# An attention and feed-forward kernel: a new table for the order and the engines of 1349 steps

## The chip, the cores and the metric

The kernel runs on one core of a Trainium2 chip. The metric is device microseconds (us) of one execution. The core has a matrix engine (PE, with its weight loads told apart as PEld), three engines for elementwise work (DVE, ACT and POOL), a sequencer that mostly issues DMA transfers (SP), and 16 DMA engines that all queues share. Each engine takes its instructions in the order in which the program gives them; between engines, semaphores hold an instruction until its operands are there.

## The reference

Linear attention with position weights comes first, then a feed-forward layer with the gate h * cos(h):

```python
r = np.maximum(x, 0.0)
phi = np.concatenate([r * cos_w, r * sin_w], axis=-1)     # for q and for k
kv = np.einsum('bhsf,bhsd->bhfd', k_p, v)
num = np.einsum('bhsf,bhfd->bhsd', q_p, kv)
den = np.einsum('bhsf,bhf->bhs', q_p, np.sum(k_p, axis=2))[..., None] + 1e-06
x = (num / den).transpose(0, 2, 1, 3).reshape(4608, 512)
h = x @ w_in                                              # 512 x 2048
out = (h * np.cos(h)) @ w_out                             # 2048 x 512
```

There are 8 batches of 8 heads, 576 rows each, 64 wide; all inputs and the output are float32.

## The kernel before

The 576 rows of a batch are laid out as 128 partitions by four and a half tiles. Tiles 0 to 3 give the 512 columns of one chunk of the feed-forward layer; the half tiles of two batches share one tile, and these rests make a ninth chunk of 512. A batch passes through these stages:

- load (L316, L319): each of k, q and v of a batch comes in by two DMA transfers on SP's queue, one of 640 KB and one of 512 KB, here called its halves (the first two batches have v in four). The raw tiles km, qm and vm exist once, so a load waits until the previous batch's work on them is done.
- prep (L343 on ACT, L344 on DVE): relu times the cosine or sine weight, from km or qm into the tile KQ, ten for k and ten for q in each batch. ENGS says which of the two engines makes each one.
- cast_v (L359 on POOL): v to 16 bits.
- kv (L370 on PE): the products of k and v into the PSUM tile ATT, copied to kvz.
- q_dma (L409 on SP): a DMA transpose of one tile of q from KQ into qT; five per batch, here called qT0 to qT4. The batches 0 and 1 use PE instead (q_pe, L399).
- num (L431 on PE, L447 to L451 on DVE): numerator and denominator, and their quotient x.
- x_dma (L481 on SP): a DMA transpose of x into xT (or xR for the rests). Batches 0 to 2 use PE (L471).
- layer 1 (L528, L560 and L664 on PE): x @ w_in, with the gate as sine on ACT (L501, L687) and product on DVE (L503, L693). L664 is part of a scheme with seven products for eight, whose sums of x (XS, L621) and of the weights (WS, L600) are made by DVE and whose partial results go through Z (L672 on ACT, L676 on DVE).
- layer 2 (L783 and L858 on PE): the product with w_out, copied to ost by ACT (L869) or added by DVE (L880), and stored by POOL (L729, L742, L746; the last chunk by SP and ACT).

Layer 1 of a chunk, layer 2 of the chunk before and the attention of a later batch run interleaved. Weights come at the start by POOL's DMA (w_in L953, w_out L967). Small copies on POOL (hold, L947, L957, L972, L979) hold back a DMA until another one has landed.

No scheduler decides the order when the program is built. Every step is registered once, with its dependencies; then a planned start (STARTS, in hundredths of a microsecond) and an engine letter (ENGS) are read from two tables:

```python
order = sorted(range(len(st)), key=lambda n: (STARTS[n], n))
...
s["fn"] = {self.LETTER[e]: o[3] for e, o in s["opts"].items()}[ENGS[s["n"]]]
return [st[n] for n in order]
```

The instructions are issued in this order, and what an engine gets of them is its queue. A planned start is thus nothing but a key to sort by. The other figures that a step is registered with (its length, its due time, the size and rate of its transfer, and how late it may land) were used by the search that made the tables; the function that runs here does not read them. In addition, steps on DVE and POOL that are marked with port=True wait for the one before them in the order when it is on the other of these two engines.

Of the kernel before, what the change touches and what calls it, by code (L numbers as in the profile page):

```python
# [11 lines left out]
ALU = mybir.AluOpType  # L12
# [6 lines left out]
    0, 53, 106, 0, 0, 71, 136, 201, 266, 331, 396, 461, 940, 1080, 1170, 990, 1662, 1904, 2064,  # L19
    1934, 607, 607, 797, 886, 733, 691, 888, 1346, 649, 669, 751, 817, 775, 731, 842, 1481, 934,  # L20
    997, 1064, 1039, 1163, 1081, 1216, 1123, 1002, 955, 940, 1191, 1126, 1258, 1225, 1165, 1284,
    1309, 1335, 1272, 1309, 1302, 1378, 1441, 1452, 1547, 1510, 1674, 1560, 1810, 1845, 1523, 1535,
    1559, 1646, 1736, 1770, 1833, 1797, 1894, 1845, 2022, 2084, 1711, 1723, 1779, 1912, 1947, 1935,
    2034, 2104, 2045, 2144, 2214, 2271, 2370, 2440, 2183, 2283, 2353, 2358, 2457, 2527, 2532, 2631,
    2701, 2445, 2544, 2614, 2619, 2719, 2789, 2794, 2893, 2995, 2707, 2806, 2934, 2881, 2980, 3056,
    3101, 3200, 3270, 3014, 3125, 3195, 3188, 3312, 3382, 3363, 3486, 3556, 3275, 3536, 3617, 2892,
    2850, 2968, 3030, 1752, 1792, 1857, 2044, 2084, 2952, 3689, 3719, 3809, 2024, 1642, 3017, 3082,
    3147, 3212, 3485, 3362, 4076, 3586, 3443, 3648, 3678, 3424, 3331, 3250, 3720, 3772, 3884, 3956,
    3762, 3710, 4148, 4218, 3846, 3884, 4102, 4194, 3888, 3983, 4363, 4490, 3804, 4119, 4318, 4375,
    4118, 3946, 4050, 4045, 3930, 4025, 4082, 4143, 4181, 4169, 4194, 4256, 4330, 4447, 4434, 4561,  # L30
    4684, 4719, 4410, 4422, 4446, 4657, 4819, 4720, 4707, 4784, 4948, 5010, 4645, 4632, 4669, 4925,
    4960, 4971, 5343, 5379, 5627, 5662, 3539, 3834, 3712, 4390, 3930, 4440, 4460, 4769, 4753, 5003,
    5455, 5671, 7278, 7188, 5170, 5816, 5824, 6060, 9378, 7368, 5083, 5182, 5526, 4996, 5095, 5178,
    5737, 5923, 5999, 5650, 5749, 5877, 5367, 5605, 5938, 6171, 6271, 6341, 5997, 6097, 6167, 6084,
    6209, 6279, 6470, 6629, 6786, 6383, 6517, 6587, 6557, 6741, 6847, 6879, 7027, 7116, 6756, 6865,
    6950, 6978, 7077, 7177, 7287, 7413, 7532, 7065, 7363, 7593, 4889, 5064, 8120, 9186, 4136, 4201,
    4331, 4266, 4396, 4461, 5232, 5356, 5484, 5281, 5480, 5239, 5418, 5294, 5323, 5542, 6030, 5860,
    5970, 6321, 6259, 6395, 5732, 5587, 5792, 5799, 5861, 5943, 5774, 6147, 6295, 5629, 5973, 6420,
    6228, 6035, 6675, 6644, 6657, 6681, 6856, 6915, 6843, 6966, 7011, 7177, 7313, 7153, 7165, 7238,
    7399, 7463, 7387, 7375, 7427, 7597, 7631, 6463, 7667, 7842, 6669, 7200, 7513, 7422, 7509, 7781,  # L40
    8356, 8262, 8522, 9043, 8002, 8917, 9155, 9288, 9375, 9726, 9487, 9661, 9787, 9866, 11601, 9834,
    9922, 10021, 11781, 11691, 7743, 7867, 7998, 7830, 7979, 8059, 7916, 8091, 8234, 8089, 8188,
    8295, 8176, 8362, 8512, 8349, 8474, 8573, 8435, 8534, 8634, 8609, 8707, 8837, 8806, 8993, 9064,
    8720, 8819, 8898, 9091, 9205, 9405, 9177, 9379, 9604, 9005, 9553, 9665, 9575, 9958, 10044, 9748,
    9846, 9983, 10034, 10195, 10295, 5562, 5627, 6545, 6610, 6165, 6230, 6965, 7385, 7189, 7127,
    6679, 6455, 7251, 7343, 6567, 6908, 7078, 6968, 7458, 7619, 7681, 8584, 7681, 7917, 7999, 8029,
    7956, 8124, 7743, 8238, 8320, 7805, 8300, 8575, 8412, 8644, 8791, 8708, 8695, 8732, 8916, 8893,
    8905, 8959, 9082, 9276, 9263, 9300, 9423, 9463, 9475, 9499, 9622, 10009, 10120, 10157, 10655,
    6402, 9125, 9848, 9922, 10483, 10691, 10988, 10145, 10487, 10601, 10877, 10977, 11453, 12461,
    11164, 11337, 11630, 11623, 11953, 12326, 11778, 12281, 12697, 12664, 12752, 13128, 14121,  # L50
    14211, 12926, 13057, 13250, 14301, 14614, 10262, 10389, 10356, 10597, 10232, 10307, 10275,
    10422, 10501, 10630, 10443, 10551, 10660, 10716, 10704, 10805, 10834, 10927, 11006, 11112,
    11064, 11294, 11392, 10574, 10766, 10866, 10747, 11244, 11331, 11493, 11680, 11783, 11251,
    11518, 11680, 11108, 11406, 11424, 11514, 11780, 12225, 11579, 11730, 11735, 11830, 11865,
    11949, 11909, 12010, 12240, 12347, 12040, 12128, 12286, 12108, 12550, 12636, 12194, 12500,
    12575, 12578, 12836, 12973, 12368, 12724, 12912, 7445, 7510, 8510, 8726, 7575, 8445, 9317, 8869,
    8470, 8931, 9429, 9491, 9603, 9093, 9255, 8757, 9578, 9468, 9318, 10381, 10319, 10878, 10133,
    9665, 10215, 9896, 10071, 10340, 9727, 10105, 10530, 10816, 10357, 10963, 10245, 10651, 11153,
    10964, 11151, 11226, 11349, 11468, 11480, 11575, 12092, 11722, 11710, 11844, 11967, 12096,
    12083, 12120, 12243, 13189, 13364, 13539, 13578, 13690, 13794, 13491, 13777, 13994, 14372,  # L60
    13951, 14094, 14299, 14566, 14853, 15094, 14436, 14678, 15228, 15248, 15422, 15666, 17419,
    17219, 15509, 15640, 15876, 15946, 16036, 12800, 12879, 12846, 13095, 12839, 12894, 12882,
    13034, 13362, 13653, 13013, 13069, 13144, 13200, 13188, 13303, 13404, 13478, 13596, 13819,
    13447, 13906, 14116, 13231, 13744, 13933, 13318, 13956, 14055, 14281, 14846, 14924, 13865,
    14560, 14652, 14050, 14106, 14237, 14311, 14734, 14985, 14194, 14249, 14392, 14448, 14523,
    14591, 14766, 14821, 15008, 15114, 14809, 14896, 15046, 15113, 15211, 15434, 14940, 15261,
    15373, 15336, 15702, 15877, 15026, 15311, 15938, 9747, 9877, 11088, 10898, 9812, 10465, 12071,
    12066, 12004, 10938, 11942, 11456, 11741, 11568, 11880, 11344, 11491, 11321, 11431, 12454,
    12516, 13412, 12944, 12774, 13026, 13300, 13119, 13382, 12438, 12662, 12744, 12178, 12758,
    13637, 12600, 12376, 14454, 13678, 13665, 13714, 13837, 14181, 14038, 14206, 14329, 14380,  # L70
    14367, 14486, 14961, 14654, 14666, 14713, 14836, 15224, 15199, 15561, 16086, 15999, 16146,
    16443, 16254, 16441, 16544, 16341, 16572, 16671, 17857, 16659, 16746, 16845, 16915, 17129,
    17161, 17862, 17987, 17317, 17516, 17801, 18080, 18167, 18534, 19296, 19206, 17949, 18255,
    18584, 18654, 18744, 19116, 20038, 15528, 15495, 15844, 16113, 15596, 15652, 15727, 15783,
    16110, 16382, 15938, 16060, 15895, 15950, 16210, 16321, 16068, 16260, 16408, 16557, 16528,
    16594, 16732, 15982, 16494, 16671, 16112, 16721, 16793, 16877, 17223, 17409, 17075, 17173,
    17243, 16833, 16957, 16963, 17027, 17441, 17796, 17032, 17273, 17273, 17329, 17473, 17735,
    17404, 17632, 17851, 17971, 18037, 18092, 18162, 17603, 17937, 18085, 17690, 18142, 18223,
    18385, 18484, 18631, 17776, 18254, 18509, 12433, 12368, 13507, 13572, 12869, 13151, 13844,
    14672, 13534, 15144, 15289, 14610, 14006, 14349, 13682, 13472, 14504, 14011, 13951, 15833,  # L80
    15771, 16000, 15361, 14946, 15443, 14784, 14498, 15086, 15814, 15752, 15896, 15331, 14882,
    16496, 16222, 16284, 17336, 16198, 16428, 16854, 16977, 17007, 17019, 17088, 17211, 17249,
    17261, 17304, 17733, 17448, 17460, 17485, 17608, 18725, 18961, 19374, 18944, 19316, 19415,
    18856, 19229, 19670, 20203, 19558, 19689, 19788, 19948, 19858, 20130, 20217, 20316, 19987,
    20373, 20940, 20787, 20874, 21110, 21574, 21484, 21048, 21135, 21234, 21394, 21304, 22607,
    22697, 18284, 18359, 18434, 18692, 18342, 18428, 18472, 18570, 18746, 18839, 18639, 18696,
    18683, 18796, 18813, 18900, 19031, 19086, 19165, 19488, 19099, 19251, 19707, 18727, 18918,
    19208, 19143, 19620, 19768, 19801, 20192, 20500, 19403, 19838, 19934, 19490, 19545, 19931,
    19995, 20242, 20647, 19645, 19720, 20086, 20142, 19887, 20317, 20304, 20378, 20579, 20708,
# [93 lines left out]
def kernel(  # L183
# [9 lines left out]
    nc = tc.nc  # L193
# [85 lines left out]
    LATE_BY, LATE_W = (0.0, 1.0, 3.0, 1.0), 0.6  # L279
# [3 lines left out]
    pl = Plan()  # L283
# [843 lines left out]
```

## Time and profile before

| what | us |
|---|---|
| median of 3 runs (lowest, highest) | 283.99 (283.96, 285.28) |
| the profiled execution | 284.86 |
| its span, from the first to the last instruction | 282.8 |
| PE busy | 270.5 (96%) |
| DVE busy | 241.8 (85%) |
| ACT busy | 208.9 (74%) |
| share of PE in the chain that ended last | 74% |
| share of DMA in that chain | 16% |
| transfers of SP's queue, as a share of 16 engines' span | 61.5% |
| transfers of POOL's queue, likewise | 29.6% |

The busy time of an engine is counted from its instructions; issuing a DMA is not counted as busy on SP, but the time that the issue takes is in the timeline. The list of waits tells for every engine and line what ended its idle time. A wait that PE doesn't see costs nothing by itself. The granted clock of PE was 1.00 throughout.

### The profile page before, as it was taken

How to read it: one execution, taken by the hardware profiler on the slowest of the kernel's cores; microseconds unless marked ns; L12 is line 12 of the kernel's file. 1: busy time of each engine (PE TensorE's matmuls, PEld its weight loads, DVE VectorE, ACT ScalarE, POOL GpSimd, SP SyncE). 2: the span in 40 equal slices, each digit the busy share in tenths (PEclk: the TensorE clock that was granted, in tenths of full speed). 3: DMA queues.
4: the chain of work that ended last, by engine and by line, in shares of the span. 5: the costliest groups of instructions: out<-in, count | busy, mean ns of one | idle time of the engine just before them, and what ended most of it. 6: DMA issues, size and time to landing. Idle time of an engine off the chain costs nothing.

```text
span 282.8 us, 6698 instructions
## 1 busy us (share of the span) xinstructions
PE 270.5 (96%) x2643; PEld 210.2 (74%) x2643; DVE 241.8 (85%) x451; ACT 208.9 (74%) x363; POOL 57.8 (20%) x87
## 2 busy tenths in 40 slices
PE   6789999999999899999999999999999999999994
PEld 2468947679955577777777787787778888776883
DVE  2975897999997789998999899999999879977752
ACT  2766897898998887798989697996555687676220
POOL 1412020030500400410042023205201360330410
PEclk9999999999999999999999999999999999999999
DMA  6999999999999979999999999959583975694424
GB/s 214 302 206 253 268 258 244 352 255 214 239 294 205 286 185 297 183 312 235 271 232 322 110 333 251 231 97 205 104 140 105 188 141 74 167 126 79 101 82 154
DMA packets 83390, 58.79 MB, mean 208 GB/s; under 512 B 46368, under 2 KB 80416, under 8 KB 83360
## 3 DMA queue, kind: packets, MB, share of 16 engines
q1 hardware_dynamic: 72128, 40.77, 61.5%
q0 software_dynamic: 10496, 17.04, 29.6%
q10 hardware_dynamic: 736, 0.57, 0.6%
q8 instruction: 20, 0.33, 0.5%
q14 instruction: 10, 0.08, 0.1%
HBM read 36.74 MB, written 11.80 MB: 172 GB/s over the span
## 4 chain that ended last, share of the span: by engine, by line
PE 74%; DMA 16%; ACT 4%; DVE 3%; issue 2%; POOL 0%; SPq 0%; DVEq 0%; POOLq 0%
PE M L858 28%; PE M L664 10%; PE M L560 10%; PE M L528 9%; DMA qT<-KQ 8%; PE TR L664 4%; PE M L783 4%; DMA w_in_sb<-in_moe_w_in_dram 3%; PE TR L560 3%; DMA km<-in_k_dram 3%; PE ATT L431 3%; PE ATT L370 2%; ACT KQ L343 2%; DMA xT<-x 2%; ACT ch L501 1%
## 5 line engine op out<-in xcount | busy, mean ns | idle before, releaser
L858 PEld LDWEIGHTS <-gT 128*128 128x128 f16 x560 | 54.2, 98 | 8.7
L501 ACT ACTIVATE ch<-M 128x512 f32<-128x512 f32 x85 | 49.6, 595 | 13.1 <-PE M L560 5.3
L503 DVE TENSOR_TENSOR gT<-M,ch 128x512 f16<-128x512 f32 x78 | 51.4, 683 | 8.1 <-ACT ch L501 8.0
L858 PE MATMUL M<-w_out_sb,gT 128*128 128x256 f16 x448 | 56.0, 273 | 0.0
L343 ACT ACTIVATE KQ<-qm,CS 128x512 f16<-128x512 f32 x55 | 37.9, 718 | 6.3 <-DMA qm<-in_q_dram 4.2
L560 PE MATMUL M<-xT,w_in_sb 128*128 128x512 f16 x160 | 38.8, 379 | 0.4 <-DVE gT L503 0.4
L343 ACT ACTIVATE KQ<-km,CS 128x512 f16<-128x512 f32 x55 | 37.6, 724 | 1.3 <-DMA km<-in_k_dram 1.3
L869 ACT ACTIVATE ost<-M 128x512 f32<-128x512 f32 x41 | 24.1, 597 | 18.4 <-PE M L858 14.5
L560 PEld LDWEIGHTS <-w_in_sb 128*128 128x128 f16 x224 | 21.4, 98 | 18.5 <-issue 0.6
L359 POOL CAST V<-vm 128x1024 f16<-128x1024 f32 (+1 forms) x18 | 16.0, 912 | 90.8 <-DVE KQ L344 27.7
L858 PE MATMUL M<-T,S 128*128 128x256 f16 x256 | 32.3, 272 | 0.0
L528 PE MATMUL M<-xT,w_in_sb 128*128 128x256 f16 x256 | 30.0, 273 | 0.6 <-DVE gT L503 0.3
L858 PEld LDWEIGHTS <-S 128*128 128x128 f16 x256 | 24.6, 98 | 4.0
L528 PEld LDWEIGHTS <-w_in_sb 128*128 128x128 f16 x256 | 24.5, 98 | 3.9 <-DVE gT L503 0.6
L664 PEld LDWEIGHTS <-w_in_sb 128*128 128x128 f16 x216 | 20.6, 98 | 3.4 <-issue 0.2
L451 DVE TENSOR_TENSOR x<-ATT,rec 128x512 f16<-128x512 f32 x32 | 22.1, 691 | 1.1
L431 PEld LDWEIGHTS <-qT 128*128 128x128 f16 x320 | 15.5, 98 | 5.4 <-DMA qT<-KQ 1.7
L729 POOL DMA_DIRECT2D out_dram<-ost x20 | 11.1, 560 | 35.3 <-ACT ost L869 19.0
L676 DVE TENSOR_TENSOR Z<-M,Z 128x512 f32<-128x512 f32 x26 | 17.7, 683 | 0.6 <-PE M L664 0.6
L672 ACT ACTIVATE Z<-M 128x512 f32<-128x512 f32 x22 | 13.1, 598 | 6.8 <-PE M L664 4.2
L431 PE MATMUL ATT<-kvz,qT 128*128 128x65 f16 x288 | 16.0, 194 | 1.7 <-DMA qT<-KQ 0.9
L664 PEld LDWEIGHTS <-WS 128*128 128x128 f16 x144 | 13.7, 98 | 4.9 <-DVE XS L621 0.9
(145 smaller groups left out, 460.6 us busy)
## 6 DMA issues: line engine op xcount, KB each, us to landing
out_dram<-ost POOLq DMA_DIRECT2D x38, 256.0 KB, 4.6
qm<-in_q_dram SPq DMA_DIRECT2D x8, 640.0 KB, 6.4
km<-in_k_dram SPq DMA_DIRECT2D x8, 640.0 KB, 7.4
qm<-in_q_dram SPq DMA_DIRECT2D x8, 512.0 KB, 6.4
km<-in_k_dram SPq DMA_DIRECT2D x8, 512.0 KB, 6.2
vm<-in_v_dram SPq DMA_DIRECT2D x6, 640.0 KB, 6.1
vm<-in_v_dram SPq DMA_DIRECT2D x6, 512.0 KB, 6.5
w_in_sb<-in_moe_w_in_dram POOLq DMA_DIRECT2D x4, 512.0 KB, 9.2
```

Source lines behind the costliest of these rows:

```text
L343: fn = {"ACT": lambda: nc.scalar.activation(out=out_, in_=in_, func=AF.Relu, scale=sc), "DVE": lambda: nc.vector.tensor_scalar(out=out_, i ...
L359: "POOL": lambda: nc.gpsimd.tensor_copy(out=out_, in_=in_)}
L431: nc.tensor.matmul(bank[hb][:, hh * D1:(hh + 1) * D1], lhsT=a[:, h, :], rhs=z[:, h, :], start=(i == 0), stop=(i == len(parts) - 1))
L451: nc.vector.tensor_tensor(out=split(x16[n][:, hs, :], k), in0=A[:, :, :, 0:D], in1=split(rec[n][:, hs], k).unsqueeze(3).broadcast_to((P, k ...
L501: act(0.5, due, lambda: nc.scalar.activation(out=ch[c], in_=bank, func=AF.Sin, bias=math.pi / 2.0, scale=1.0), [key], [("ch", c)])
L503: mul(due, 0.61, lambda q: q.tensor_tensor(out=dst, in0=bank if len(dst.shape) == 2 else bank.rearrange("p (j s) -> p j s", j=dst.shape[1] ...
L528: nc.tensor.matmul(M1[m][:, jj * 2 * P:(jj + 1) * 2 * P], lhsT=w_in_sb[:, cc, j * P:(j + 1) * P], rhs=X[:, cc, ts], start=(cc == 0), stop= ...
L560: nc.tensor.matmul(M, lhsT=w_in_sb[:, cc, j * P:(j + 1) * P], rhs=X[:, cc, :], start=(cc == 0), stop=(cc == NCT - 1))
L664: nc.tensor.matmul(bank[0][:, j * TH:(j + 1) * TH], lhsT=a(cc, j), rhs=b[:, cc, :], start=(first and j == 0 and cc == 0), stop=(last and j ...
L676: dve(0.61, due + 0.3, lambda: nc.vector.tensor_tensor(out=dst, in0=bank[0], in1=dst, op=ALU.add), [bank[1], key], [key])
L858: nc.tensor.matmul(bank[0][:, tt * MH:(tt + 1) * MH], lhsT=a[:, j, tt * P:(tt + 1) * P], rhs=b[:, j, :], start=(first and (apart or tt == ...
L869: act(0.5, due, lambda: nc.scalar.activation(out=dst, in_=view(bank), func=AF.Copy), [bank[1]], dk)
```

## The change

Two tables change, and with them the order on each engine; the functions register the same 1349 steps, and the program has the same instructions. Of the steps, 38 preparations change their engine: 22 from DVE to ACT and 16 from ACT to DVE. PE keeps 422 steps, POOL 81 and SP 111, in another order. The changed figures of length (0.9 to 0.55 and 1.2 to 0.9 for a DMA that POOL issues, 0.65 to 0.62 for a store by SP) and LATE_BY are those that the search read. A limit on what SP's queue can hold was part of the search and does not stand in the code.

```diff
 STARTS = (
-    0, 53, 106, 0, 0, 71, 136, 201, 266, 331, 396, 461, 940, 1080, 1170, 990, 1662, 1904, 2064,
...
+    53, 106, 0, 0, 74, 139, 204, 269, 334, 399, 464, 543, 1050, 1190, 1280, 1100, 1370, 2014, 2134,
...
 ENGS = (
...
-    "ADPADPADPADPADPADDDDDSSSSSSAADDADAADAGGGPPADDSAASDASDASDASPPDPAPPDPAPPDPAPPDPADDDPPAPPDDPP"
+    "ADPADPADPADPADPADDDDDSSSSSSDDADADAADAGGGPPADASAASDASAASAASPPDPAPPDPAPPDPAPPDPADDDPPAPPDDPP"
...
-    LATE_BY, LATE_W = (0.0, 1.0, 3.0, 1.0), 0.6
+    LATE_BY, LATE_W = (0.0, 0.8, 1.8, 0.5), 0.6
...
-        pl.add(eng, 0.9 if eng == "POOL" else 0.65, 0, due, lambda: q.dma_start(out=dst, in_=src_), keys, [], dma=(nb, 355.0))
+        pl.add(eng, 0.55 if eng == "POOL" else 0.62, 0, due, lambda: q.dma_start(out=dst, in_=src_), keys, [], dma=(nb, 355.0))
```

The order on SP's queue from the loads of batch 4 to the last transpose of batch 3 shows the kind of change (kA and kB, qA and qB, vA and vB are the halves of batch 4; the qT of the first column are those of batch 3, but for qT4 of batch 2 where it says so):

```
before: qT4 of batch 2, kA, kB, vA, qT0, qT1, qT2, vB, qA, qT3, qB, qT4, four xT
after:  kB, qT4 of batch 2, qT0, vA, kA, qT1, vB, qT2, qA, qT3, qB, qT4, four xT
```

On POOL, the four loads of w_in now follow each other at once, and the four stores of chunk 0 (L729) stand together around the last cast of v of batch 3; before, three stood there and the fourth stood with the casts of batch 4.

## The prediction

> **What bounds the kernel now.** I read the page first, then the table of stretches, then the chain of waits, and last what PE and SP waited for between 74 and 140 us. All times are those of one profiled execution: 284.86 us, of which the span is 282.8 and 2.06 lie around it. It is 0.87 above the median of the three runs, 283.99.
>
> ```profile
> PE 270.5 (96%) x2643; PEld 210.2 (74%) x2643; DVE 241.8 (85%) x451; ACT 208.9 (74%) x363; POOL 57.8 (20%) x87
> ```
>
> PE is the bound, busy for 96% of the span. The stretches show where the rest lies (columns: PE, PEld, DVE, ACT, POOL busy with instructions in brackets, clock, DMA share, GB/s).
>
> ```profile
> 60.00:80.00 20.00, 20.00 (x262) 17.25 (x260) 18.70 (x36) 17.85 (x34) 5.95 (x9) 1.00 1.05 230
> 80.00:100.00 20.00, 18.59 (x144) 11.55 (x142) 16.99 (x33) 17.81 (x33) 3.15 (x4) 1.00 1.11 281
> 100.00:120.00 20.00, 19.37 (x206) 15.11 (x205) 18.63 (x35) 15.94 (x29) 3.28 (x5) 1.00 0.97 213
> 120.00:140.00 20.00, 19.45 (x195) 15.01 (x193) 18.65 (x33) 18.42 (x34) 1.38 (x3) 1.00 1.14 278
> 140.00:180.00 40.00, 40.00 (x416) 32.40 (x414) 37.84 (x72) 34.37 (x60) 10.41 (x16) 1.00 1.17 258
> 180.00:220.00 40.00, 40.00 (x385) 31.55 (x383) 38.48 (x67) 28.05 (x50) 8.16 (x12) 1.00 0.75 132
> ```
>
> PE idles in the head (to 36 us), at the tail (after 277.1), and between 80 and 140 us; outside these it is full, so there no order of the other engines can gain anything. The idle of 80 to 140 us is four waits, told by the list of waits:
>
> ```profile
> PE ATT L431 <- DMA qT<-KQ: 0.9, 1, 0.9
> PE M L664 <- DVE XS L621: 0.6, 1, 0.6
> PE M L664 <- ACT Z L672: 0.5, 1, 0.5
> ...
> PE M L560 <- DVE gT L503: 0.4, 1, 0.4
> ```
>
> In order of time they end at 87.42 (L560), 97.28 (L431), 107.87 and 134.41 us (L664) and last 0.44, 0.91, 0.63 and 0.55. Behind each stands a transfer of SP's queue. DVE came late to the first for a half of k (the same list: DVE KQ L344 waited 0.9 for km, to 86.28 us), the second is a transposed q, the third a transposed x (DVE XS L621 waited 1.0), the fourth began with ACT waiting 1.3 for a qT. SP's rows show why:
>
> ```profile
> 71.46 2.06 SPq L409 DMA_TRANSPOSE qT<-KQ  x1
> ...
> 75.71 1.55 SPq L316 DMA_DIRECT2D km<-in_k_dram  x1
> ...
> 80.69 8.08 SPq L409 DMA_TRANSPOSE qT<-KQ  x3
> ...
> 90.29 3.16 SPq L409 DMA_TRANSPOSE qT<-KQ  x1
> ...
> 96.64 3.08 SPq L481 DMA_TRANSPOSE xT<-x  x2
> ...
> 132.31 1.24 SPq L409 DMA_TRANSPOSE qT<-KQ  x1
> ```
>
> A transpose is issued in 1.24 us where nothing stands ahead of it (last line), and often in 2 to 4 us from 64 to 125 us (8.08 for three): SP can't hand over the next one until earlier transfers have gone. The DMA engines' share there is 1.11 and 1.14.
>
> **The change part by part.** *The numbers in the code.* Only STARTS and ENGS act on the program: run() sorts by STARTS. The costs, LATE_BY and the room of the queue act on nothing that is built. Cost 0; PE has the same 2643 matmuls.
>
> *What can be won.* Each wait also empties PE's pipe: a 128x256 matmul lasts 273 ns, but eight take 0.87 us, 109 ns each, so a gap costs 0.16 more than it shows. The four are worth 0.60, 1.07, 0.79 and 0.71, together 3.17 us.
>
> *Engines.* Of the head preparations 22 go from DVE to ACT and 16 back: ACT gains 6 x 0.72 = 4.3 us, DVE loses 6 x 0.49 = 2.9. I cost this at 0. ACT's idle 74 us cover it; without that cover (17.81 of 20 busy from 80 to 100 us) a preparation on ACT holds up the sines of L501 queued behind it, 0.72 each.
>
> *Head.* POOL issues the fourth w_in load with the others (11 to 14 us, before 17.44), and the holds of the next raw loads follow it; the second q half and the v loads are issued up to 7 us earlier, behind k loads that are still under way. What PE waits for stays: w_in (first L528 at 20.75) and w_out (L783 at 36.17). I take 0. Bounds: a gain of 0.6 (the waits of 0.28 and 0.32 at 20.75 and 23.20), a loss of 0.74 (one POOL issue of w_in more ahead).
>
> *First wait (0.60).* The qT4 of batch 2 goes from 71.46 to behind the first half of the next k, and the second half of that k, before next to the first, now follows qT4, qT0 and a v half. Before, the halves landed 9.4 and 10.4 us after their issue, the last at 86.1. Two more transfers (qT0, v) now precede the last. In the full queue from 80.69 to 96.53 eight transfers were issued in 15.84 us, 1.98 each; unhindered, a transpose takes 1.24 and a load 0.60. So that half lands at 86.3 + 1.84 = 88.1 to 86.3 + 3.96 = 90.2. The new table sets its first use (now ACT) 1.96 us later than before; a group of eight matmuls counts 0.87 there as in the rows, so I read this as 1.96 us of PE work done first. Against the old wait that is -0.1 to +2.0; I take +0.6, below the middle, since ACT's other preparations can run ahead. Behind it in ACT's queue stand a copy of L869 and the sines that DVE's L503 needs, and PE waits for L503. This wait: 1.2, from 0.5 to 2.6.
>
> *Second wait (1.07).* It is for qT3 of batch 3. Ahead of it in SP's queue since 71 us are the same nine transfers, in another order, and all four stores of POOL now stand at 72 to 74 us, where three stood (the fourth was at 95.60). PE comes later to it by the first wait's growth. I take 0.5; bounds 0 and 1.07 + 0.93 = 2.0 (256 KB at 281 GB/s for the fourth store).
>
> *Third wait (0.79).* The x transposes keep their place behind qT4; only the loads behind them change order. They start when DVE's x is there. I take 0.2, near the row of an unhindered xT (2.8 to 3.3 us to land), bounds 0 and 0.79.
>
> *Fourth wait (0.71).* qT4 of batch 4 goes behind the first x transpose, three more x transposes follow it, then the next k. It landed 8.82 us after its issue; the median is 5.5. The table leaves 6.2 between issue and the preparation that overwrites its source. I take 0.3; bounds 0 and 8.82 - 6.2 = 2.6, halved to 1.3 since ACT is behind PE by less than its wait.
>
> *Later.* From 140 us PE never waited. SP's transfers move by up to 9 us in the table there, a k half of batch 6 again parts from its twin. New waits: 0.2, bounds 0 and 1.0. The tail keeps its 5.7 us from 277.1 on.
>
> *Sum.* 1.2 + 0.5 + 0.2 + 0.3 + 0.2 = 2.4 in place of 3.17: 0.8 gained, 284.06 for an execution like the profiled one, and 0.87 less for the median: 283.2.
>
> While the three stores were under way (8.7 to 9.4 us from issue to landing), the qT issued at 71.46 took 10.2 us to land; the k halves of the batch before, with no store beside them, took 4.1 and 5.2. [...]
>
> **The rivals.** *SP is on time.* The new order leaves more work between issue and use; then only the first wait's lower end, 0.5, stays: 283.99 - 2.67 = 281.3. For it: all four waits are SP's, and the queue is not full after 125 us. Against: the DMA share of 1.11, which an order can't lower.
>
> *Nothing moves.* The DMA engines are full, not SP's handing over; the same bytes land when they did and the waits keep their sum of 3.17: 284.0. For it: the nine transfers ahead of qT3, and the burst of four stores, which may take back at qT3 what is won before it. [...] Against: between 100 and 120 us the share is 0.97, and a wait is there all the same.
>
> *Slower: the parted k.* The second half of k lands at 90.2, ACT stands still 2.0 longer than DVE did, and the other three waits stay: 283.99 + 2.0 = 286.0. It decides when that half lands later than 86.3 + 1.96 = 88.2, and passes 0.5% from 89.7 on. For it: 9.4 and 10.4 us to landing in this very place. Against: ACT has other work that could fill the time, if its order lets it.
>
> **How the numbers follow.** Half a per cent (1.42 us) is about what a measurement of this kernel can tell from no change: faster is below 282.57, slower above 285.41. My sum 0.35 (its own range 282.2 to 284.2, a sixth of it below 282.57), SP on time 0.22, nothing moves 0.25, the parted k 0.18. Faster: 0.22 + 0.06 + 0.02 = 0.30. Slower: 0.16 + 0.01 = 0.17. Same: 0.53. The range leaves half of the fast rival below 281.5 and half of the slow one above 285.8.
>
> **What would show it.** Each step by its wait: at about 88 us ACT L343 waiting for km (right) or DVE (wrong); qT landing for L431 near 97; XS L621 waiting under 0.4 for xT; no PE idle from 140 to 277 us. If SP's transposes between 76 and 97 us take 1.3 us each, SP is on time and I am too slow; if PE idles in the head or in a stage that was full, I am too fast.

## The result and the profile after

| | median, us | range, us | ratio to the kernel before, 95% interval |
|---|---|---|---|
| before, 22 runs | 284.37 | 281.02 to 286.70 | |
| changed, 22 runs | 286.42 | 284.28 to 288.47 | 1.009 (1.0065 to 1.0114) |

The changed kernel is 0.9% slower. Forecast were 283.2, a range of 281.5 to 285.8, and a chance of 0.17 for slower. (Intervals here leave out executions more than 1.5% above the fastest of their kernel; medians and means keep them.)

The profiled execution of the changed kernel took 284.28 us (span 282.5): the shortest of its 22. Read alone, it agrees with the forecast (284.06 for an execution like the profiled one). Its busy line, and its stretches in the columns shown for before:

```profile
PE 270.9 (96%) x2643; PEld 210.1 (74%) x2643; DVE 241.0 (85%) x445; ACT 213.0 (75%) x369; POOL 57.7 (20%) x87
```

```profile
60.00:80.00 20.00, 19.96 (x260) 17.20 (x259) 18.08 (x36) 18.21 (x33) 5.40 (x8) 1.00 1.08 288
80.00:100.00 20.00, 19.68 (x158) 12.47 (x157) 18.77 (x34) 17.52 (x33) 2.61 (x3) 1.00 1.10 241
100.00:120.00 20.00, 19.16 (x200) 15.05 (x199) 18.20 (x33) 17.89 (x32) 0.95 (x2) 1.00 1.03 198
120.00:140.00 20.00, 19.93 (x200) 15.54 (x199) 19.28 (x35) 18.14 (x32) 4.31 (x7) 1.00 1.11 287
140.00:180.00 40.00, 39.36 (x407) 31.41 (x405) 36.28 (x69) 35.03 (x61) 9.95 (x15) 1.00 1.10 248
```

PE's idle time from 80 to 140 us fell from 2.59 to 1.23 us, and 0.64 is new between 140 and 180. The list of waits names what PE waited for; the first two lines lie in the head:

```profile
PE M L399 <- ACT KQ L343: 2.6, 1, 2.6
PE ATT L942 <- POOL S L928: 1.3, 1, 1.3
PE ATT L431 <- DMA qT<-KQ: 1.2, 2, 0.8
PE M L858 <- ACT ost L869: 0.6, 1, 0.6
```

The timeline of SP's queue, and ACT's use of the parted half of k:

```profile
75.69 5.22 SPq L409 DMA_TRANSPOSE qT<-KQ  x2
...
81.67 0.63 SPq L319 DMA_DIRECT2D km<-in_k_dram  x1
...
104.71 7.99 SPq L409 DMA_TRANSPOSE qT<-KQ  x3
```

```profile
86.98 1.33 ACT L343 ACTIVATE KQ<-km,CS 128x512 f16<-128x512 f32 x2 [0.32 <-DMA km<-in_k_dram]
```

SP needs 2.6 us for a transpose in these rows, against 2.7 in the row of 80.69 before, and 1.5 to 3.5 between 82 and 95 us, so SP hands them over about as slowly as it did. But what PE needs lands in time more often: the half of k issued at 81.67 is there at 86.98, after a wait of ACT of 0.32, and PE doesn't see it. So this profile shows a gain, and 22 executions show a loss. The experiments look for what this profile leaves out.

### The profile page after: what moved, and what is told of

It is laid out like the page before. It is cut to its first block, busy times and chain, and to the rows that moved or that the text cites. A ratio compares the mean times of both kernels' runs of the same rounds, so it can differ in the third digit from the quotient of the medians.

```text
span 282.5 us, 6678 instructions
## 1 busy us (share of the span) xinstructions
PE 270.9 (96%) x2643; PEld 210.1 (74%) x2643; DVE 241.0 (85%) x445; ACT 213.0 (75%) x369; POOL 57.7 (20%) x87
## 4 chain that ended last, share of the span: by engine, by line
PE 47%; DMA 4%; DVE 2%; ACT 2%; issue 0%; POOL 0%; ACTq 0%; DVEq 0%
PE M L858 24%; PE M L664 8%; PE M L560 7%; DMA out_dram<-ost 4%; PE TR L664 4%; PE TR L560 2%; PE ATT L431 1%; ACT ost L869 1%; PE ATT L370 1%; DVE ost L880 1%; ACT KQ L343 0%; DVE gT L503 0%; POOL out_dram L729 0%; ACT ch L501 0%; DVE ost L922 0%
## 5 line engine op out<-in xcount | busy, mean ns | idle before, releaser
L858 PEld LDWEIGHTS <-gT 128*128 128x128 f16 x560 | 54.1, 98 | 8.4
L503 DVE TENSOR_TENSOR gT<-M,ch 128x512 f16<-128x512 f32 x78 | 52.3, 684 | 7.0 <-ACT ch L501 6.5
L858 PE MATMUL M<-w_out_sb,gT 128*128 128x256 f16 x448 | 56.7, 273 | 0.0
L343 ACT ACTIVATE KQ<-qm,CS 128x512 f16<-128x512 f32 x59 | 40.5, 718 | 4.2 <-DMA qm<-in_q_dram 4.2
L343 ACT ACTIVATE KQ<-km,CS 128x512 f16<-128x512 f32 x57 | 39.3, 717 | 2.6 <-DMA km<-in_k_dram 2.6
L858 PE MATMUL M<-T,S 128*128 128x256 f16 x256 | 32.3, 272 | 0.6 <-ACT ost L869 0.6
L858 PEld LDWEIGHTS <-S 128*128 128x128 f16 x256 | 24.7, 98 | 5.4 <-issue 0.9
L729 POOL DMA_DIRECT2D out_dram<-ost x20 | 10.8, 542 | 58.9 <-ACT ost L869 48.0
L431 PEld LDWEIGHTS <-qT 128*128 128x128 f16 x320 | 15.7, 98 | 6.6 <-DMA qT<-KQ 2.7
L431 PE MATMUL ATT<-kvz,qT 128*128 128x65 f16 x288 | 16.3, 194 | 1.8 <-DMA qT<-KQ 1.2
L746 POOL DMA_DIRECT2D out_dram<-ost x12 | 7.0, 588 | 48.2 <-ACT ost L869 48.2
```

The source lines that it names most:

```text
L343: fn = {"ACT": lambda: nc.scalar.activation(out=out_, in_=in_, func=AF.Relu, scale=sc), "DVE": lambda: nc.vector.tensor_scalar(out=out_, i ...
L431: nc.tensor.matmul(bank[hb][:, hh * D1:(hh + 1) * D1], lhsT=a[:, h, :], rhs=z[:, h, :], start=(i == 0), stop=(i == len(parts) - 1))
L503: mul(due, 0.61, lambda q: q.tensor_tensor(out=dst, in0=bank if len(dst.shape) == 2 else bank.rearrange("p (j s) -> p j s", j=dst.shape[1] ...
L858: nc.tensor.matmul(bank[0][:, tt * MH:(tt + 1) * MH], lhsT=a[:, j, tt * P:(tt + 1) * P], rhs=b[:, j, :], start=(first and (apart or tt == ...
```

## The experiments

### Both kernels once more, and half a table

The kernels `again_before` and `again_after` are the two kernels unchanged. The other two join the tables at 60 us (in kernels whose table is written anew, STARTS holds ranks, which sort alike, and line numbers are 22 lower: L377 is L399):

```diff
 b60a
-order: all steps by STARTS (new), engines by ENGS (new)
+order: steps with STARTS (old) < 6000 in the old order with the old engines,
+       then all others by STARTS (new), ENGS (new)
 a60b
+order: steps with STARTS (new) < 6050 in the new order with the new engines,
+       then all others by STARTS (old), ENGS (old)
```

> The kernel before, once more, for a second trace and the granted clock of its runs. Late transfers: PE stands still for SP's transfers by more in this execution than the 3.2 us of the first one in some executions, less in others; the clock is as in the runs of the new table. Clock: the granted clock is 0.998 or more in nearly all runs, where the new table's runs had 0.993 in the mean (0.986 to 1.000).

> The new table, once more. The first trace of it was the fastest of its 22 runs (284.28 against a median of 286.42), so this one should be slower. Late transfers: PE idles between 36 and 277 us by 4 to 6 us in a median execution (2.9 in the first trace), and what ends its waits are qT, xT or a late k, q or v. Clock: the waits are as in the first trace, and matmuls take 0.5 to 1% longer in stretches of lower clock, 1.5 to 2 us in all.

> The order and engines of before for all that its table starts before 60 us (head, batches 0 and 1, first loads of batch 3), then the new table. Late transfers: most of the loss is in the steady stages, so ratio to before 1.006 to 1.010. If the loss is made in the head: 0.998 to 1.002. Clock: as the new table, 1.006 to 1.010.

> The new table until 60.5 us, then the order and engines of before. Late transfers: ratio to before 0.998 to 1.003. If the loss is made in the head: 1.006 to 1.010. Clock: as before, 0.998 to 1.002.

| kernel | median, us (before: 283.85) | ratio, 95% interval | mean clock |
|---|---|---|---|
| again_before | 284.55 | 1.0027 (0.9997 to 1.0058) | 0.9956 |
| again_after | 286.18 | 1.0069 (1.0034 to 1.0103) | 0.9973 |
| b60a | 285.26 | 1.0040 (1.0008 to 1.0072) | 0.9968 |
| a60b | 286.05 | 1.0076 (1.0042 to 1.0111) | 0.9932 |

The loss is there again, at a mean clock no lower than that of the kernel before: the clock alone is not its cause. The new order of the first 60 us brings all of it even where the old order follows, which points to the head, where I had costed the change at nothing. b60a's 0.4% could be the seam's; the two mixtures together lose more than the changed kernel (0.40 and 0.76%, against 0.7 to 0.9%), so a part of a60b's loss can be its seam's too.

### The parts of the change, one by one

Four mixtures: SP's 111 steps in one kernel's order and the rest in the other's (`a_spb`, `b_spa`), and one kernel's order with the other's engine letters (`be_a`, `ae_b`).

```diff
 a_spb: STARTS (new), ENGS (new)
+       SP's steps in the order of STARTS (old)
 b_spa: STARTS (old), ENGS (old)
+       SP's steps in the order of STARTS (new)
 be_a:  STARTS (old)
-       ENGS (old)
+       ENGS (new)
 ae_b:  STARTS (new)
-       ENGS (new)
+       ENGS (old)
```

> The changed kernel with one thing put back: SyncE's 111 steps are issued in the order of the kernel before (62 places differ); TensorE's order differs from the changed kernel's in 14 places, VectorE's in 18, ScalarE's in 62, GpSimd's in none, and the letters are the new ones. So far the changed kernel is 1.9 us (0.7 to 0.9%) over the kernel before, at the same granted clock, though its profiled executions are not longer: something that varies from one execution to the next costs it more. Theory 'SyncE's room': it is SyncE's transfers, whose first uses now come 8.8 us after the issue instead of 10.8 for the q transposes; then the old queue order gives most of the loss back: 284.0 to 284.8, ratio 1.000 to 1.003, and in its profile no TensorE wait on qT, kA or xT over 0.6 us. Theory 'compute order': the loss is in how TensorE, VectorE and ScalarE are ordered among themselves; then this stays at 285.7 to 286.4, ratio 1.006 to 1.009. Theory 'letters': as for compute order, and the two runs on the letters decide.

> The kernel before with one thing changed: SyncE's 111 steps are issued in the changed kernel's order (62 places differ); TensorE's order differs from the kernel before in 27 places, VectorE's in 47, ScalarE's in 76, GpSimd's in none, letters as before. Theory 'SyncE's room': this alone carries the loss, 285.3 to 286.4, ratio 1.005 to 1.009, with a new TensorE wait on a transpose's result in its profile. Theory 'compute order' and theory 'letters': 283.6 to 284.6, ratio 1.000 to 1.003.

> The kernel before with its order of planned times and the changed kernel's 38 other engine letters (22 evictions from VectorE to ScalarE, 16 the other way). Theory 'letters': the loss is here, 285.3 to 286.4, ratio 1.005 to 1.009. Theories 'SyncE's room' and 'compute order': small, 283.8 to 284.9, ratio 1.000 to 1.004 (an eviction out of its planned place may cost some tenths).

> The changed kernel's order with the engine letters of the kernel before. Theory 'letters': the loss goes, 283.8 to 284.8, ratio 1.000 to 1.003. Theories 'SyncE's room' and 'compute order': 285.7 to 286.8, ratio 1.006 to 1.010.

| kernel | median, us (before: 283.75) | ratio, 95% interval |
|---|---|---|
| a_spb | 297.62 | 1.0488 (1.0426 to 1.0551) |
| b_spa | 292.22 | 1.0332 (1.0279 to 1.0384) |
| be_a | 288.36 | 1.0184 (1.0135 to 1.0232) |
| ae_b | 288.61 | 1.0176 (1.0128 to 1.0224) |

All four are slower than both kernels, so they tell nothing about which part carries the loss: an order of PE, a queue of SP and a set of letters fit each other, and a mixture pays for the mismatch, 14 us at worst. In a_spb, PE has waits behind the head that neither kernel's profiles show, above all one of 3.1 us that ends at 180.3 us and one of 1.3 that ends at 146.3 (the first two lines; L836 is L858 of the unedited kernels, L409 is L431):

```profile
PE M L836 <- ACT ost L847: 3.1, 1, 3.1
PE ATT L409 <- DVE x L429: 1.6, 2, 1.3
PE M L642 <- DVE gT L481: 1.5, 3, 0.6
```

### More profiles of the changed kernel

The kernels `look1` to `look3` are the changed kernel, unedited; `a140b` is a60b with the seam at 141 us.

```diff
 a140b
-order: all steps by STARTS (old), ENGS (old)
+order: steps with STARTS (new) < 14100 in the new order with the new engines,
+       then all others by STARTS (old), ENGS (old)
```

> The changed kernel unchanged, for one more profiled execution: both so far (spans 282.5 and 281.7) were the shortest of their 22 and 12, and their TensorE gaps of 6.29 and 5.67 us are less than the 6.81 and 7.93 of the kernel before, so they don't show the 1.9 us that the median lost. In an execution near the median (span 284.5) some 2 us more are idle on TensorE. Theory 'SyncE's room': the new gaps are at waits on qT, kA or xT, or on a VectorE result of which the chain leads to a SyncE transpose, between 80 and 180 us. Theory 'compute order': at waits on ScalarE or VectorE results (KQ, ost, gT) with no late transfer behind them. Theory 'loads': at waits on w_in or w_out in batches 0 to 2, or on x or v. A mean clock under 0.99 in the profile would mean that this execution says little.

> As the look before it: the same kernel, another profiled execution. The gaps over 0.5 us that come back in both are of the kernel; those in one alone are of the execution.

> As the two looks before it. If all three are again at spans under 283, the profiled executions are not like the others, and the traces can't show where the 1.9 us are.

> The changed kernel's order and letters for the steps planned before 141 us, and after it the order and letters of the kernel before. Theory 'SyncE's room', whose late transfers in the profiles seen lie before 150 us: the whole loss stays, 285.5 to 286.4, ratio 1.006 to 1.009. If half the loss is made after 141 us (TensorE waits 0.4 to 1.2 us for an eviction at 171 to 174 us in three of the profiles, and b60a lost 0.4%), 284.6 to 285.3, ratio 1.003 to 1.005, plus what the seam costs.

The medians of look1 to look3 are 286.92, 285.92 and 286.22 (before: 283.75; ratios 1.0113, 1.0086 and 1.0070, the intervals from 1.0058, 1.0049 and 1.0027 up), a140b's is 286.57, ratio 1.0098 (1.0065 to 1.0131): again the whole loss comes with the earlier part of the new table. The profiled spans are 285.5, 283.7 and 285.2, and now the loss can be seen. First the stretches of the head, in the profiled execution of the section above and then in look3:

```profile
5.00:9.00 4.00, 1.35 (x11) 0.57 (x9) 1.67 (x5) 1.70 (x3) 0.00 (x0) 1.00 1.07 358
9.00:12.50 3.50, 3.50 (x41) 2.44 (x39) 3.02 (x7) 2.19 (x5) 1.53 (x3) 1.00 1.09 359
12.50:16.00 3.50, 3.09 (x48) 1.94 (x47) 3.30 (x10) 2.88 (x7) 1.93 (x3) 1.00 1.06 181
```

```profile
5.00:9.00 4.00, 1.70 (x6) 0.50 (x4) 0.28 (x1) 0.31 (x1) 0.00 (x0) 1.00 1.02 323
9.00:12.50 3.50, 2.36 (x23) 2.39 (x24) 2.24 (x6) 2.38 (x5) 0.33 (x2) 0.53 1.06 366
12.50:16.00 3.50, 3.50 (x18) 1.89 (x16) 3.50 (x9) 3.08 (x7) 3.34 (x4) 0.50 0.71 136
```

The column behind POOL is the granted clock: in look3 it is 0.50 from 9.2 to 16.0 us, and PE gets through 41 matmuls between 9 and 16 us where the first has 89. The timelines of ACT (first) and PE in look3 show the other half; a line of PE in the profile of before follows them:

```profile
8.69 1.95 ACT L343 ACTIVATE KQ<-qm,CS 128x512 f16<-128x512 f32 x3 [5.58 <-DMA qm<-in_q_dram]
```

```profile
5.55 1.14 PE L942 MATMUL ATT<-S 128*128 128x512 f16 x4
10.14 1.86 PE L399 MATMUL M<-IDENT,KQ 128*128 128x128 f16 x16 [3.44 <-ACT KQ L343]
...
20.09 0.42 PE L431 MATMUL ATT<-kvz,qT 128*128 128x65 f16 x8 [0.52 <-DVE kvz L384]
```

```profile
8.65 1.07 PE L399 MATMUL M<-IDENT,KQ 128*128 128x128 f16 x16 [2.73 <-ACT KQ L343]
```

The first q is prepared at 8.69 us, not at 7.30 as in the changed kernel's first profile, so PE starts on it (L399) at 10.14 instead of 8.75, and at half clock it needs 9.95 us instead of 7.48 to the first numerator (L431).

| execution | first q on ACT | L399 | L431 | from L431 to PE's last matmul |
|---|---|---|---|---|
| before (two) | 7.26, 7.46 | 8.65, 8.84 | 16.15, 16.35 | 262.7, 263.1 |
| changed, first two | 7.30, 7.31 | 8.75, 8.75 | 16.23, 16.28 | 262.3, 261.5 |
| look1 | 9.38 | 10.83 | 20.34 | 261.2 |
| look2 | 8.22 | 9.67 | 18.19 | 261.5 |
| look3 | 8.69 | 10.14 | 20.09 | 261.1 |

On the mean of its five profiles the changed kernel comes to L431 1.98 us later (18.23 against 16.25): 0.88 from the later start of L399, and 1.09 from the way to L431, which takes 7.5 us at full clock, 8.5 in look2 and 9.5 and 9.95 in the others. Behind the head it is 1.35 us faster in these profiles (261.5 against 262.9). The two parts don't add up to the loss: these five have a mean span of 283.7 and the two of before 283.1, only 0.6 apart, where all executions are 2.3 apart, so the 1.35 is in part the draw of these seven executions. Little of a late start comes back there: against the fastest execution, again_after, the three come to L431 4.1, 1.9 and 3.8 us late and end 3.8, 2.0 and 3.5 late.

The falls last 3.4 us (9.2 to 12.6 in look2) or 6.8 (9.0 to 15.8 in look1, 9.2 to 16.0 in look3). The same program has one in the head of these three executions and none in the head of its first two profiles.

### The memsets, and the clock

Up to 7 us the two kernels differ in one thing alone: VectorE's first three steps, memsets (L987) of a half tile each of q, k and v, are in the order v, q, k in the new table. The second half of q's load (L316) waits for q's memset: it is issued at 1.56 us where that memset ends at 1.43, and at 2.00 where it ends at 1.97. VectorE's memset of q, before and then after:

```profile
0.95 0.48 DVE L987 MEMSET qm<- 128x512 f32 x1
...
1.49 0.48 DVE L987 MEMSET qm<- 128x512 f32 x1
```

The timelines of SP, before and then after:

```profile
0.74 0.76 SPq L319 DMA_DIRECT2D qm<-in_q_dram  x1
1.56 0.62 SPq L316 DMA_DIRECT2D qm<-in_q_dram  x1
2.22 0.64 SPq L319 DMA_DIRECT2D km<-in_k_dram  x1
```

```profile
0.74 0.76 SPq L319 DMA_DIRECT2D qm<-in_q_dram  x1
2.00 0.62 SPq L316 DMA_DIRECT2D qm<-in_q_dram  x1
2.67 0.64 SPq L319 DMA_DIRECT2D km<-in_k_dram  x1
```

`a_qkv` and `b_vqk` turn this order round in each kernel (keys of steps 0 to 4); `a_warm` and `b_warm` let PE multiply on while it waits for q:

```diff
 a_qkv
-    53, 106, 0, 0, 74, ...
+    0, 53, 106, 0, 74, ...
 b_vqk
-    0, 53, 106, 0, 0, ...
+    53, 106, 0, 0, 0, ...
 a_warm, b_warm
-        warm(14, 6.5)
+        warm(22, 6.5)
```

> The changed kernel with three steps put back: VectorE's first three memsets of the fifth token are of q, k, v again (the new table has v, q, k). In every profile with v first SyncE issues the second half of q at 2.00 us instead of 1.56 and all loads behind it 0.44 us later. The first eviction of q starts at 7.2 to 7.6 us in the five profiles with q first, and at 7.2, 7.2, 7.8, 8.1, 8.1, 8.6, 8.6, 9.3 and 9.3 in the nine with v first; in six of the nine the granted clock falls to 0.5 for 3.4 to 7 us from about 9 us, in none of the five. The three looks at the changed kernel lost 1.9 to 4.05 us in the first 16 us and kept them. Theory 'memset order': this is the loss; q's eviction comes at 7.2 to 7.6 us again, no clock below 0.99, and the time is 283.0 to 284.3, ratio 0.996 to 1.002. Theory 'head, but by chance': the load's lateness has nothing to do with the order, the time stays at 285.7 to 286.4, ratio 1.006 to 1.010. Theory 'no reserve' (the loss is made later, where a late transfer finds no wait to hide in): the same 285.7 to 286.4.

> The kernel before with its first three memsets in the new table's order, v, q, k, and nothing else changed. Theory 'memset order': later q, the clock at 0.5 near 9 us in half the executions; if the later waits of the kernel before don't hide it, 285.0 to 286.2, ratio 1.004 to 1.009; if they hide it, 284.0 to 284.6 with waits at 87 to 134 us that are shorter by what the head lost. Theories 'by chance' and 'no reserve': 283.6 to 284.4, ratio 0.999 to 1.002, L399 at 8.7 us.

> The changed kernel with 22 matmuls instead of 14 in the first group of TensorE, whose results nothing reads; at 0.2157 us each at full clock it ends 1.7 us later, at 7.9 to 8.7 us, before q's first eviction is through (8.7 us at the earliest). TensorE stands idle for 1 us there instead of 2.7 to 4.25. Theory 'clock': the falls to 0.5 near 9 us go (clock 0.997 and over in all executions) and the time falls by what they cost, about 1 us on average: 284.9 to 285.5, ratio 1.003 to 1.006, and the rest of the loss is elsewhere (q late by 1 us on average). If the clock falls all the same, or the time stays at 286.2 without them, the fall of the clock is not what costs.

> The kernel before with the same 22 matmuls. Its executions at a clock of 0.994 are no longer than those at 1.000 (282.1 against 282.15 us of span), so its later waits hide what the clock costs or its clock falls where TensorE waits anyway: 283.6 to 284.3, ratio 0.998 to 1.002, clock 0.997 and over. If the head is passed on in this kernel too, 283.0 to 283.6.

| kernel | median, us (before: 284.32) | ratio, 95% interval | mean clock |
|---|---|---|---|
| a_qkv | 285.76 | 1.0047 (1.0012 to 1.0083) | 0.9949 |
| b_vqk | 285.23 | 0.9984 (0.9936 to 1.0032) | 0.9944 |
| a_warm | 285.67 | 1.0051 (1.0019 to 1.0082) | 0.9978 |
| b_warm | 286.28 | 1.0081 (1.0043 to 1.0119) | 0.9954 |

*Memsets.* Over all profiles of this study the first q is prepared at 7.15 to 7.73 us in the eight with q's memset first, and at 7.30 to 9.41, on the mean 8.34, in the twelve with v's first; the means differ by 0.95 (the times in the expectation above are up to 0.1 lower than the timelines'). a_qkv itself shows 7.15. L431 starts at 16.15 to 17.30 us, on the mean 16.5, in the six with q's memset first and the first group of 14 matmuls, and at 16.23 to 20.74, on the mean 18.4, in the ten such with v's first. In time, a_qkv's mean span is 283.86 against 284.61 of 50 executions of the changed kernel, 0.75 less, and b_vqk's 283.16 against 282.30 of 125 of the kernel before, 0.86 more. The kernel before was slower when these four were measured, 282.61 on the mean of 35 executions; set against that, a_qkv gains 1.06 (1.25 above before, where the changed kernel is 2.31 above) and b_vqk loses 0.55. Neither is shown by itself: a_qkv's interval meets that of the changed kernel, and b_vqk's executions spread so far (281.03 to 287.83) that its ratio leaves out six of twelve and says nothing. I take the memsets for some 0.8 us, a third of the loss, by the two together and the shift in the profiles. a_qkv did not reach the 283.0 to 284.3 that my theory asked for, and its profile has a fall of the clock, from 8.5 to 11.9 us, although q is early.

*Clock.* a_warm's mean clock rises from 0.9940 to 0.9978, its mean span falls by 0.9 to 283.72, and its median is just above the 284.9 to 285.5 expected. But it does not take the fall away: its profile still has one, from 10.8 to 14.2 us. Nor is the clock the cause for the most part. Of executions at 0.9975 and over, 14 of the changed kernel have a mean span of 284.1 and 54 of the kernel before 282.0: 2.1 us apart, of 2.3 over all. A fall of 3.4 us to half lowers the mean clock of such an execution by 0.006 (my estimate, 3.4 x 0.5 / 282). Between 0.9895 and 0.9955, about one fall, lie 46% of the changed kernel's executions and 44% of those before; below that 18% and 2%. So falls are somewhat more frequent with the new table, and long ones much more.

*b_warm* fell out of every theory. PE starts on q at 8.70 as before, and yet the kernel is 2 us slower. Its profile shows two waits of 1.5 us close together, and the clock falling to 0.5 from 90.4 to 93.8 us, during the second of them; the waits, then the stretches:

```profile
PE M L560 <- DVE gT L503: 1.5, 1, 1.5
PE ATT L431 <- DMA qT<-KQ: 1.5, 1, 1.5
```

```profile
85.00:90.00 5.00, 3.08 (x18) 1.50 (x16) 2.75 (x5) 3.23 (x7) 0.00 (x0) 1.00 1.26 242
90.00:94.00 4.00, 2.89 (x15) 1.35 (x16) 1.66 (x4) 1.37 (x4) 0.00 (x0) 0.57 1.02 200
```

In this profile a wait of PE of 1.5 us in mid-kernel thus goes with 3.4 us at half the clock. Why eight matmuls in an idle stretch make these waits longer stays open.

### The same head for both

`a_late` and `b_late` make TensorE's first group so long that q, in every profile so far, is there before it ends: a late load or a fall near 9 us should not show in the head any more. In their profiles L399 starts at 13.50 and 13.77 us and L431 at 20.63 and 20.90, and the mean clock is 0.999 and 1.000.

```diff
-        warm(14, 6.5)
+        warm(44, 6.5)
```

> The changed kernel with 44 matmuls instead of 14 in the first group of TensorE. At 0.2157 us each at full clock the group ends 30 x 0.2157 = 6.5 us later, at 12.4 to 13.3 us, when q's first evictions are through in every profile seen (8.7 to 10.9 us). So the head is the same in the two kernels of this pair and in all executions: TensorE starts on q some 3.7 us later than in an undisturbed execution of either, whatever the load of q does, and it is never idle before, so the clock has no reason to fall. What differs between this one and the next is only what comes behind the head. Theory 'head' (the loss of the changed kernel is made in its first 16 us alone): this one is 0 to 1.4 us faster than the next. Theory 'no reserve' (the kernel before gets a late start back in its waits at 87 to 134 us, the changed kernel has none to give): this one keeps 3.2 us or more of the 3.7, 286.5 to 288.5, and is 0.5 to 2 us slower than the next.

> The kernel before with the same 44 matmuls. Theory 'no reserve': of the 3.7 us it gets 1.5 to 2.5 back where TensorE waits for transfers that the late start doesn't move (3.2 us of such waits in its first profile, 0.9 us in its fastest relative): 285.3 to 286.8, and in its profile the waits at 87 to 134 us sum to under 1 us. Theory 'head': the waits stay, because what they wait for is late with the head: 287.3 to 288.3, with 2 to 3 us of waits at 87 to 134 us.

| kernel | median, us (before: 283.58) | ratio, 95% interval | mean span |
|---|---|---|---|
| a_late | 288.34 | 1.0169 (1.0134 to 1.0204) | 286.47 |
| b_late | 288.09 | 1.0129 (1.0076 to 1.0182) | 285.65 |

With the same head the two are 0.25 us apart in their medians, 0.8 in their mean spans and 1.1 by their ratios, where the unedited kernels are 2.0 to 2.4 apart. That points to the head for about half of the loss or more. With six executions each the difference has a standard error of 0.9 us, and the intervals overlap, so it bears this out only together with the 1.98 us of the profiles. Neither theory got its numbers: a_late is not faster than b_late, as 'head' asked for, and b_late is not below 286.8, as 'no reserve' did. The theory 'no reserve' has its traces, though. PE's lists of waits, a_late and then b_late:

```profile
PE ATT L431 <- DMA qT<-KQ: 2.5, 3, 1.0
```

```profile
PE M L664 <- DVE gT L503: 1.5, 1, 1.5
...
PE M L664 <- ACT Z L672: 0.5, 1, 0.5
```

Against the first profile of before, b_late starts L399 5.1 us late and is only 1.6 late at 108 us: it takes back 3.5, where PE used to wait for transfers. Then it loses 1.5 again at 135 us. Against again_after, a_late starts 4.7 late, has 2.7 left at 53 us, and waits for qT at 94, 97 and 170 us, so that it ends 5.5 late. Whether the changed kernel takes back less in general, two profiles and six executions of each can't settle: against the changed kernel's first profile the same a_late ends 4.6 late.

## Why the prediction was wrong

*What bounds the kernel*: right. PE is busy for 96% before and after.

*Numbers in the code, engines*: no run contradicts the 0; be_a and ae_b show only that letters and order can't be parted. ACT's busy time grew by 4.1 us, near the 4.3 worked out, but DVE's fell by 0.8 and not by 2.9.

*Head*: this is the step that failed, "I take 0. Bounds: a gain of 0.6 [...], a loss of 0.74". It measured +1.98 us in the mean of five profiles, and a60b, with the new order up to 60 us alone, loses 0.76%, where the changed kernel loses 0.7 to 0.9%. The step looked at weights and at the later loads, and concluded that what PE waits for stays. It left out the very first wait of all, of L399 for q, and the three memsets ahead of it, although the diff shown ends up with them in its first line: `0, 53, 106` became `53, 106, 0`. The new order issues half of q's load 0.44 us later, and q is then prepared 0.95 later on the mean over the profiles; some 0.8 us of the time hang on it, by runs of which neither shows it alone. The fall of the clock in the head was in no list of mine, since the profile of before showed 1.00 throughout. Of the changed kernel's executions 36% have a mean clock of 0.9925 or less (look1 to look3 have 0.988 to 0.991), of those before 9%.

*First wait*, 1.2 forecast: 0 in all five profiles. The parted half of k is used 5.3 us after its issue in the first of them and 5.8 in look3; before, the halves took 9.4 and 10.4 to land. So my estimate of 88.1 to 90.2 was too late; with it fell the slower rival that had its chance. *Second wait*, 0.5: 0.32, 0, 0.85, 0 and 1.81, on the mean 0.6: right in size, over a wide spread. A wait for another qT at 112 us, 0.83 and 0.25 in two of the profiles, was in none of my steps. *Third and fourth*, 0.2 and 0.3: none. *Later*, 0.2 with a bound of 1.0: 0 to 1.6, on the mean 0.9, above all L858 behind ACT's ost, at 143 to 146 and 171 to 175 us, and two waits for qT at 148 and 165 us; mis-sized. Together PE's waits from 80 to 180 us are 1.7 on the mean, some 2.1 with 0.16 for PE's pipe at each (273 less 109 ns a matmul, the prediction's estimate); 2.4 were forecast, and the kernel before had 2.5 and 3.4, 3.2 and 3.8 so counted. In these profiles the waits shrank as the steps said, and by more; whether that is the order's doing isn't shown, as the next paragraph tells.

*From one execution to the median*: also wrong. I took the 3.17 us of one execution for what there is to win. Its span, 282.8, and that of the second profile, 283.4, are above the mean of 125, 282.30; b_vqk, which has the order of before behind the head, shows waits of 0.9 us in this place and a span of 280.5. So part of the four waits was, it seems, that execution's own, and an order can't win it. The changed kernel's first profile erred the other way.

*Rivals.* "SP on time" fell: between 76 and 97 us the transposes of q take 2.4 us each to issue on the mean (1.5 to 3.5), not 1.3. "Nothing moves" fell by its time, 284.0. Its mechanism stays open: the sum of the waits is smaller in the profiles of the changed kernel, with four stores in the burst, but b_vqk's 0.9 with three is smaller still, and no run tests the burst by itself. The slower side came true, by none of the mechanisms that I had, so the chance of 0.17 that it got is no merit of the working.

*Still open*: why q's load lands up to 2 us later for an issue 0.44 later. In the eight profiles with the first q at 8.2 us or later the DMA engines moved 253 to 355 GB/s from 5 to 7 us, in the twelve others 357 to 380, so the transfers themselves were slower; what slowed them no run shows. Open is also what makes the part of the loss that is neither the memsets' nor the clock's, some 0.6 to 1.3 us of the 2.3.

## What to carry to other kernels

When a diff reorders everything, read its first steps as carefully as the stage where the profile shows waits: here one memset more ahead of half of the first load put that half and the loads behind it 0.44 us later, and look1 to look3, which were 4.1, 1.9 and 3.8 us late at L431, ended 3.8, 2.0 and 3.5 us late. One profiled execution is a draw from a spread (here 5 to 6 us wide); a wait of half a microsecond in it may be the execution's and not the kernel's, so a forecast for the median needs several profiles or wide bounds. Parts of a searched order can't be put together singly: each mixture of one kernel's queue or letters with the other's order lost more than either kernel, 1.8 to 4.9%.

## What the runs showed of the hardware

The granted clock fell to 0.50 in the head of eight profiles (look1 to look3, a140b, a_spb, ae_b, a_qkv and a_warm) for 3.4 or 6.8 us, from between 8.5 and 10.8 us on, during or just behind gaps of PE of 2.2 to 4.3 us. It fell at a gap of 2.23 us in a_qkv (from 8.5 us on) and not at one of 3.42 us in a60b, so the length of a gap alone doesn't decide it in these runs. What goes with it is the time at which the first matmuls change their pace from 0.43 to 0.215 us: in the sixteen profiles with 14 matmuls in the first group that is at 3.9 to 4.7 us in the nine without a fall in the head, and at 5.1 to 6.4 in the seven with one, which comes 3.3 to 3.5 us behind it. a_qkv fell with an early q and the change at 5.1. Six of the ten with v's memset first have the late change and the late q together; why, no run shows. A fall costs 1.0 to 1.3 us on the way from L399 to L431 when it is short and 2.0 to 2.5 when it is long. In the profile of before the change of pace comes at 4.2 us, in look3 at 5.9; the granted clock reads 1.00 ahead of it all the same, so the 1.00 "throughout" of the profile before stands beside both paces.
